# Group-major table A, column-tiled picking and a second buffer for table B in an S4 + GLU kernel

## The chip, the cores and the metric

One core of one Trainium2 chip. The metric is the device time of the kernel in microseconds (us), median over the runs. Fast runs of one kernel agree within about 1% here. Each run is put into a state (fast or slow); only fast runs are compared below. TensorE is called PE, VectorE DVE, ScalarE ACT, GpSimd POOL; "the clock" is the TensorE clock that was granted, 1.00 being full speed.

## The reference

The input is 2048 rows of 640 channels (D), with N = 128 complex states in each channel. Cut to what matters here:

```python
P = jnp.exp(logdA[:, :, None] * l[None, None, :])          # D x N x L powers
K = jnp.einsum("dn,dnl,dn->dl", Cc, P, dB).real             # the convolution's kernel, 640 x 2048
Kf, Uf = rfft2(pad(K)), rfft2(pad(u.T))
y = irfft2(Uf * Kf)[..., :L] + u * Dskip                    # u is the layer-normed input
h = x + y
out = h + (sigmoid(ln(h) @ w_gate) * (ln(h) @ w_up)) @ w_down   # D 640, F 1728
```

The change touches only how K is made.

## The kernel before

K is made in two halves of 320 channels. A tap index l is split as l = b + 8a: table B holds 21 values of b, already multiplied by C·dB, and table A holds the 32 powers of 8a. DVE builds both with chains of complex multiplies (`chain_a`, `chain_b`), the 128 states on the partitions. Then, for each group of four channels, one matrix product over the states gives every a and b at once: 128 weights (32 entries of A x 4 channels), 84 moving columns (21 entries of B x 4 channels), twice, for the real and the imaginary part. Of its result only the entries with equal channels are wanted; matmuls with one-hot weights ("picks") gather them from the evicted tile `kts` into `kv`.

```python
T["A"] = tabp.tile([P, 2, 32, w], BF16, name="tabA")        # entry, then channel; w = 320
T["B"] = tabp.tile([P, 2, 21, w], BF16, name="tabB")        # one buffer
# ... (cut)
Av = [T["A"][:, ri].rearrange("p a (c g) -> p (a c) g", c=4) for ri in range(2)]
Bv = [T["B"][:, ri].rearrange("p b (c g) -> p (b c) g", c=4) for ri in range(2)]

def product(g1, kts):                                        # kts: [P, 84, GC], GC = 20 groups
    for g0 in range(0, GC, 5):
        pk = psk.tile([P, 5, 84], F32, name="pk", tag="k")
        for i in range(5):
            for ri in range(2):
                nc.tensor.matmul(pk[:, i, :], lhsT=Av[ri][:, :, g1 + g0 + i], rhs=Bv[ri][:, :, g1 + g0 + i], ...)
        nc.scalar.copy(kts[:, :, g0:g0 + 5].rearrange("p x g -> p g x"), pk[:])

def diagonal(g1, kts):
    for c in range(4):
        # ... (cut)
        for m in range(4):                                   # 128 output columns, accumulated
            nc.tensor.matmul(pv, lhsT=pick[:, c, m, :], rhs=kts[:, 4 * m + c:4 * m + c + 65:16, :], start=(m == 0), stop=(m == 3))
        nc.tensor.matmul(ps[0:4, 1, 0:GC], lhsT=last[:, c, :], rhs=kts[:, 80 + c, :], start=True, stop=True)
        nc.scalar.copy(kvv[:, :, c, g1:g1 + GC], pv)
        nc.vector.tensor_tensor(kl[:, dc], ps[0:4, 1, 0:GC], uh[:, dc], ALU.mult)
```

Channel d is stored as (c, g) with c in 0..3 and g in 0..79, so neighbouring weights of a group lie 80 bf16 elements (160 bytes) apart, and so do neighbouring moving columns. The eviction writes each bf16 40 bytes from the last (GC = 20). The picks read `kts` in dense runs of 20.

The order of work is: tables of half 0, product of half 0, tables of half 1 with the spectrum of half 0 (`kspec`), product of half 1, spectrum of half 1, MLP.

## Time and profile before

557.67 us, median of 3 runs (555.96 to 559.83). The first view is the table of windows of the kernel before. Each line is one stretch: its length, the busy time of PE, of PE's weight loads, of DVE, ACT and POOL (in brackets the instructions), the granted clock, the DMA share and GB/s.

```profile
core 0: us, PE busy (x) PEld busy (x) DVE busy (x) ACT busy (x) POOL busy (x), PEclk, DMA share, GB/s
0.00:100.20 100.20, 31.73 (x146) 14.79 (x147) 87.13 (x144) 74.31 (x132) 20.52 (x25) 0.96 0.47 147
100.20:145.80 45.60, 40.69 (x260) 32.88 (x260) 6.75 (x26) 41.35 (x43) 0.67 (x2) 0.50 0.12 33
145.80:225.80 80.00, 51.01 (x369) 28.53 (x367) 75.72 (x98) 23.82 (x39) 0.00 (x0) 0.76 0.55 158
225.80:265.80 40.00, 37.58 (x240) 31.78 (x240) 2.42 (x16) 33.57 (x32) 0.00 (x0) 0.50 0.09 19
265.80:555.70 289.90, 251.91 (x1405) 125.81 (x1427) 122.03 (x237) 61.08 (x99) 5.20 (x8) 0.93 0.26 87
```

| stretch | what it is | what sets its length |
|---|---|---|
| 0 to 100.2 | tables of half 0, layer norm, first transform of u | DVE, 87.1 of 100.2 us busy |
| 100.2 to 145.8 | product and picking, half 0 | PE 40.7 and ACT 41.4 of 45.6 us; the clock is 0.50 |
| 145.8 to 225.8 | tables of half 1, spectrum of half 0 | DVE, 75.7 of 80 us |
| 225.8 to 265.8 | product and picking, half 1 | PE 37.6, ACT 33.6 of 40 us; the clock is 0.50 |
| 265.8 to 555.7 | spectrum of half 1, loads, MLP | not touched |

The instructions of the two products stand in these groups (line, engine, operation, tiles, shapes, count; then busy us and mean ns of one; then the idle time before them and what ended it):

```profile
L378 ACT CAST kts<-pk 128x420 bf16<-128x420 f32 x32 | 62.8, 2081 | 9.8 <-PE pk L377 9.3
L377 PE MATMUL pk<-tabB,tabA 128*128 128x84 bf16 x320 | 59.6, 353 | 11.4 <-DVE tabB L312 6.3 <-ACT kts L378 4.9
...
L385 PE MATMUL ps_kv<-kts,c_pick 128*128 128x100 bf16 x128 | 17.7, 279 | 2.1 <-DVE klast L389 2.1
```

A mean time of a matmul is not its cost, because matmuls overlap. Their cost is read from the timeline of PE, from one start to the next:

```profile
112.78 1.87 PE L377 MATMUL pk<-tabB,tabA 128*128 128x84 bf16 x10 [0.85 <-ACT kts L378]
115.50 3.73 PE L377 MATMUL pk<-tabB,tabA 128*128 128x84 bf16 x20 [0.84 <-ACT kts L378]
119.04 0.43 PE L385 MATMUL ps_kv<-kts,c_pick 128*128 128x100 bf16 x3
...
130.78 0.44 PE L385 MATMUL ps_kv<-kts,c_pick 128*128 128x100 bf16 x3
131.15 0.18 PE L386 MATMUL ps_kv<-kts,c_last 128*4 128x20 bf16 x1
131.26 0.51 PE L385 MATMUL ps_kv<-kts,c_pick 128*128 128x100 bf16 x4
131.70 0.18 PE L386 MATMUL ps_kv<-kts,c_last 128*4 128x20 bf16 x1
...
140.03 0.27 PE L385 MATMUL ps_kv<-kts,c_pick 128*128 128x100 bf16 x1
140.23 0.18 PE L386 MATMUL ps_kv<-kts,c_last 128*4 128x20 bf16 x1
```

Twenty product matmuls take 119.04 - 115.50 = 3.54 us to the next start, 177 ns each.

### The profile page before, as it was taken

The page shows a single profiled execution, that of the slowest core. Times are in us where ns is not written, and L with a number is a line of the kernel's source. Part 1 is how long each engine was busy: PE and PEld are TensorE (multiplying, and loading weights), DVE is VectorE, ACT ScalarE, POOL GpSimd, SP SyncE. Part 2 cuts the span into 40 slices and gives each one's busy share as a digit, 9 for nine tenths or more (in the row PEclk, how much of TensorE's full clock was granted, in tenths as well). Part 3 has the DMA queues.
Part 4 walks back from the last instruction along what each step waited for, and adds up shares of the span by engine and source line. Part 5 has one row for each costly group of instructions (what it writes and reads, how often), then busy time and mean ns, then how long its engine had stood idle before and what let it go on. Part 6 is the DMA issues. An engine that isn't in the chain of part 4 may idle for free.

```text
span 555.7 us, 6282 instructions
## 1 busy us (share of the span) xinstructions
PE 412.9 (74%) x2417; PEld 233.8 (42%) x2440; DVE 294.1 (53%) x518; ACT 234.1 (42%) x341; POOL 26.4 (5%) x35
## 2 busy tenths in 40 slices
PE   1201734789655885699968359799979999999997
PEld 1100212578423453587534124444444444444443
DVE  4899899400589999200653275732273236322321
ACT  5679866889601364598445203030202110311210
POOL 0721200000000000000000000000000000000000
PEclk9999998555557898555799669799988999999999
DMA  7330546500253477001798991200100010001001
GB/s 207 124 115 30 195 176 177 141 1 2 58 142 94 139 239 226 14 1 16 255 297 281 276 385 55 94 1 1 48 0 1 1 47 1 0 1 47 2 8 40
DMA packets 47725, 54.73 MB, mean 98 GB/s; under 512 B 6928, under 2 KB 39760, under 8 KB 47696
## 3 DMA queue, kind: packets, MB, share of 16 engines
q1 hardware_dynamic: 47696, 54.33, 31.3%
q8 instruction: 19, 0.31, 0.2%
q14 instruction: 10, 0.08, 0.1%
HBM read 41.21 MB, written 13.11 MB: 98 GB/s over the span
## 4 chain that ended last, share of the span: by engine, by line
PE 49%; DVE 27%; ACT 9%; DMA 9%; issue 2%; POOL 2%; SPq 1%; POOLq 0%; DVEq 0%; ACTq 0%
PE ml_pg L605 11%; PE ml_po L619 10%; PE ml_pu L605 10%; PE pk L377 7%; DVE tS L310 5%; ACT kts L378 5%; PE ps_xk L417 4%; DMA mk<-s4c_M 4%; DVE ln_st L216 3%; DVE tabB L311 3%; DVE u L235 2%; PE ps_kv L385 2%; DMA W2g<-s4c_W 2%; DVE tabB L312 2%; DVE h L478 2%
## 5 line engine op out<-in xcount | busy, mean ns | idle before, releaser
L607 ACT ACTIVATE ml_sg<-ml_pg 128x512 bf16<-128x512 f32 (+1 forms) x56 | 33.3, 597 | 120.9 <-PE ml_pg L605 120.9
L608 DVE TENSOR_TENSOR ml_hm<-ml_pu,ml_sg 128x512 bf16<-128x512 f32 (+1 forms) x56 | 38.7, 691 | 78.8 <-PE ml_pu L605 69.7
L605 PE MATMUL ml_pg<-lnT,Wg 128*128 128x512 bf16 (+1 forms) x273 | 71.3, 391 | 0.5 <-issue 0.2
L605 PE MATMUL ml_pu<-lnT,Wu 128*128 128x512 bf16 (+1 forms) x274 | 69.1, 380 | 0.5 <-issue 0.4
L377 PE MATMUL pk<-tabB,tabA 128*128 128x84 bf16 x320 | 59.6, 353 | 11.4 <-DVE tabB L312 6.3
L378 ACT CAST kts<-pk 128x420 bf16<-128x420 f32 x32 | 62.8, 2081 | 9.8 <-PE pk L377 9.3
L619 PE MATMUL ml_po<-Wd,ml_hm 128*128 128x512 bf16 (+3 forms) x438 | 64.8, 298 | 0.6 <-issue 0.2
L417 PE MATMUL ps_xk<-kv,mk 128*128 128x320 bf16 x340 | 57.2, 328 | 10.0 <-DMA mk<-s4c_M 8.9
L377 PEld LDWEIGHTS <-tabA 128*128 128x128 bf16 x320 | 50.1, 162 | 18.6 <-issue 15.4
L418 ACT CAST xk<-ps_xk 128x640 bf16<-128x640 f32 x34 | 23.5, 693 | 65.0 <-PE ps_xk L417 49.8
L417 PEld LDWEIGHTS <-mk 128*128 128x128 bf16 x340 | 34.7, 106 | 31.8 <-DMA mk<-s4c_M 11.0
L619 PEld LDWEIGHTS <-ml_hm 128*128 128x128 bf16 x448 | 33.3, 97 | 31.8 <-issue 9.0
L605 PEld LDWEIGHTS <-Wg 128*128 128x128 bf16 (+1 forms) x280 | 27.8, 101 | 35.3 <-issue 6.5
L605 PEld LDWEIGHTS <-Wu 128*128 128x128 bf16 (+1 forms) x280 | 27.6, 99 | 31.8
L389 DVE TENSOR_TENSOR klast<-ps_kv,uhead 4x20 bf16<-4x20 f32 x32 | 4.8, 166 | 65.4 <-ACT kv L387 65.4
L621 DVE TENSOR_TENSOR ml_out<-ml_po,h 128x640 bf16<-128x640 f32 x16 | 13.2, 825 | 42.8 <-PE ml_po L619 42.8
L591 ACT COPY lnT<-ml_pt 128x512 bf16<-128x512 bf16 x8 | 4.7, 586 | 61.6 <-PE ml_pt L590 61.6
L332 PEld LDWEIGHTS <-c_F_99 128*128 128x128 bf16 x64 | 8.0, 126 | 51.7 <-issue 47.5
L449 ACT CAST g_stg<-ps_g 128x640 bf16<-128x640 f32 x32 | 21.0, 699 | 10.1 <-PE ps_g L445 7.5
L352 PEld LDWEIGHTS <-W2g 128*64 128x64 bf16 x136 | 10.0, 156 | 33.4 <-DMA W2g<-s4c_W 20.1
L478 DVE TENSOR_TENSOR h<-ps_y,h 128x640 bf16<-128x640 f32 x16 | 12.8, 819 | 13.9 <-PE ps_y L474 12.7
L310 DVE TENSOR_TENSOR tS<-tabA,tabMA 128x3200 bf16<-128x3200 bf16 (+3 forms) x14 | 19.5, 1393 | 0.7 <-ACT tabA L302 0.4
(346 smaller groups left out, 547.4 us busy)
## 6 DMA issues: line engine op xcount, KB each, us to landing
mk<-s4c_M SPq DMA_DIRECT2D x34, 320.0 KB, 3.8
d1u<-s_stg SPq DMA_DIRECT2D x16, 320.0 KB, 2.6
a2g<-d1u SPq DMA_DIRECT2D x16, 320.0 KB, 3.2
W3g<-s4c_W SPq DMA_DIRECT2D x16, 192.0 KB, 3.6
u<-in_A_u_dram SPq DMA_DIRECT2D x4, 640.0 KB, 6.3
d_0_58<-g_stg SPq DMA_DIRECT2D x8, 320.0 KB, 3.6
h<-in_A_u_dram SPq DMA_DIRECT2D x4, 640.0 KB, 8.1
d_1_59<-g_stg SPq DMA_DIRECT2D x8, 320.0 KB, 4.2
```

The costliest lines, as they stand in the source:

```text
L216: nc.vector.bn_stats(st[:, r, hh, :], src[:, r, 320 * hh:320 * hh + 320])
L310: nc.vector.tensor_tensor(t, X[:, :, src, :], mm, ALU.mult)
L377: nc.tensor.matmul(pk[:, i, :], lhsT=Av[ri][:, :, g1 + g0 + i], rhs=Bv[ri][:, :, g1 + g0 + i], start=(ri == 0), stop=(ri == 1))
L378: nc.scalar.copy(kts[:, :, g0:g0 + n].rearrange("p x g -> p g x"), pk[:, 0:n, :])
L417: nc.tensor.matmul(ps[:, ri, 0:w], lhsT=mk[:, ri, j, :], rhs=kv[:, j, :], start=(j == 0), stop=(j == 4))
L418: nc.scalar.copy(xk[:, qi, :, :], ps[:, :, 0:w])
L449: nc.scalar.copy(stg[0][:, 2 * (q % 2):2 * (q % 2) + 2, :], ps[:, :, 0:w])
L478: nc.vector.tensor_tensor(hv, ps[:, :, 0:w], hv, ALU.add)
L605: nc.tensor.matmul(ps[0:fw, :], lhsT=W[:, dc, f0:f0 + fw], rhs=rhs, start=(dc == 0), stop=(dc == 4))
L607: nc.scalar.activation(sg[0:fw, :], pg[0:fw, :], AF.Sigmoid)
L608: nc.vector.tensor_tensor(hm[0:fw, ft, :], pu[0:fw, :], sg[0:fw, :], ALU.mult)
L619: nc.tensor.matmul(po[:, c0:c0 + w], lhsT=hm[0:fw, ft, 128 * lr:128 * lr + 128], rhs=Wd[0:fw, ft, c0:c0 + w], start=(ft == 0), stop=(ft == ...
```

## The change

The intent: let every access of the product be dense. A is laid out group by group, so that a group's 128 weights are side by side. B keeps its rows, but the four channels of a group become neighbours, so the moving operand comes in runs of four. The eviction then writes a group's 84 values side by side. The picking reads at steps instead (168 bytes), so it is recast: 16 matmuls with 32 output columns each, four of them beside each other in the PE array, writing PSUM at steps of 16 bytes; one eviction of 400 columns for 20 groups in place of four of 100. B gets two buffers, so that half 1's chain B can run while half 0's product still reads B. The rest of the diff regroups and reorders work: chain A does its multiplies in fewer, larger steps, the complex product C·B and some small steps of the layer norm go from POOL to DVE, the second transform of u for half 1 is evicted by ACT instead of DVE, and chain B, chain A, the spectrum and the transform are interleaved. The core of the diff:

```diff
+    bp = sc.pool("tabb", bufs=2, side="right")
...
-        T["A"] = tabp.tile([P, 2, 32, w], BF16, name="tabA")
-        T["B"] = tabp.tile([P, 2, 21, w], BF16, name="tabB")
+        A = T["A"] = tabp.tile([P, 2, w // 4, 32, 4], BF16, name="tabA")
+        T["B"] = bp.tile([P, 2, 21, HALVES[hf][1]], BF16, name="tabB", tag="B")
...
-                        nc.tensor.matmul(pk[:, i, :], lhsT=Av[ri][:, :, g1 + g0 + i], rhs=Bv[ri][:, :, g1 + g0 + i], ...)
-                nc.scalar.copy(kts[:, :, g0:g0 + n].rearrange("p x g -> p g x"), pk[:, 0:n, :])
+                        nc.tensor.matmul(pk[:, i, :], lhsT=A[:, ri, g].rearrange("p e c -> p (e c)"), rhs=B[:, ri, :, 4 * g:4 * g + 4], ...)
+                nc.scalar.copy(kts[:, g0:g0 + 5, :], pk[:])
...
-                for m in range(4):
-                    nc.tensor.matmul(pv, lhsT=pick[:, c, m, :], rhs=kts[:, 4 * m + c:4 * m + c + 65:16, :], start=(m == 0), stop=(m == 3))
-                nc.scalar.copy(kvv[:, :, c, g1:g1 + GC], pv)
+                for m in range(4):
+                    nc.tensor.matmul(pv[32 * m:32 * m + 32, :, :, c], lhsT=pick[:, c, :], rhs=kj[:, :, :, 4 * m + c], start=True, stop=True,
+                                     tile_position=(0, 32 * m))
+            nc.scalar.copy(kv[:, :, 4 * g1:4 * g1 + 4 * GC], ps[:, 0, 0:20 * GC].rearrange("p (j x) -> p j x", j=5))
...
+    open_b(1)
+    nc.scalar.copy(T["B"][:, :, 0, :], CB1[:])
+    kv = kmm(0, ktp, kx, T0)
+    cb = chain_b(1)
+    drain(cb, 4)
+    ks, s2 = kspec(0, kv, xu0, kw2, mkp, False), u_s2(1, xu1, a2p, nc.scalar.copy)
+    for _ in range(5):
+        drain(cb, 1); drain(ks, 1); drain(s2, 1)
...
```

## The prediction

> **What bounds the kernel now.** From 337 us on (219 us) it is the MLP: PE 94% busy at clock 0.97 (table of windows); the change does not touch it. Before, by windows and timeline:
> - 0–100 us: VectorE (DVE) builds tables A and B of half 0, busy for 87 of 100 us; the first product waits for the last tabB add (100.3).
> - 100–145 and 226–266: products and diagonal picking. Ten product matmuls take 1.87 us, the ACT eviction of each five groups 2.08 us (128x420, written at steps of 40 bytes; a dense 128x640 takes 0.69). The two leapfrog at clock 0.50. DVE does 6.5 and 1.2 us of work: idle.
> - 145–226: DVE builds half 1, evicts u_s2 (17 at 0.82 us) and multiplies the spectrum: 76 of 81 us busy. It sets the start of the second product.
> - 266–316: spectrum of half 1, waiting on mk loads.
>
> **What the change does.**
> 1. Product: a group's 128 weights are dense, B comes in runs of four, the eviction is dense: 0.55 us (estimate from 0.69). A dense pair (picking, 100 columns) takes 0.112 us at clock 0.5 today, so I estimate 1.1 us per ten matmuls. Sixteen blocks per half: 18 us.
> 2. Picking: still 20 matmuls per block of 20 groups, now 32-column tiles side by side, reading SBUF at steps of 168 bytes and writing PSUM at 16. Today 2.2 us. The Trainium skill (Advanced Engine Details and Errata, Memory Cachelines) says non-contiguous PSUM patterns slow matmuls; no trace here shows how much. I take 2.5 us, tiles overlapping. With it a half takes about 29 us, against 45 and 40.
> 3. Chain A keeps its elements (28 us by today's durations) if runs of four bf16 keep two elements per cycle. The skill (Vector Engine (DVE) Microarchitecture Reference, 5.1 and 5.2) asks for an innermost step of one and runs of 8 bytes; these satisfy it.
> 4. B in two buffers: about 11 us of half 1's chain B moves under the first product; not more, because the DVE queue holds four klast multiplies that wait for the picking. The u_s2 eviction (13 us) moves to ACT, which has room. The 81 us become about 58: 12 chain B, 2.5 bases, 28 chain A, 13 spectrum, waits.
> 5. Front: GpSimd work that stretched eight u normalisations to 8.75 us (the later eight: 2.94) goes; but CB moves to DVE (about 7 us) and half 1's B bases come earlier. Net about zero.
>
> **Sum.** First product 99, its end 128, second product 186, its end 215 (now 265.7): 50 us saved, all on the critical path. Spectrum of half 1, weight loads and MLP follow unchanged (290 us).
>
> Predicted 508 us, range 492 to 528. Faster by over 2%: 0.94; within 2%: 0.04; slower: 0.02.
>
> **What the profile would show.** Step 1: kts eviction 0.5–0.6 us, ten matmuls about 1.1 us, no wait of PE on ACT. Step 2: picking block 2–3 us. Step 3: DVE 2240- and 2560-element multiplies near 1.3 and 1.5 us. Step 4: DVE busy in the first product; second product near 186, released by the last tabA add. Step 5: u normalisation near 0.37 us each. MLP 219 us.
>
> **What would make it wrong.** Chain A at one element per cycle: plus 25 us per half, which eats the gain. Picking serialised by PSUM steps: plus up to 25 us. A clock above 0.5 in the denser product: minus up to 14. The spectrum of half 0 with u_s2 (about 13 MB of loads and stores) DMA-bound in 58 us.

## The result and the profile after

The changed kernel takes 470.38 us, median of 4 runs (467.87 to 471.65); the kernel before in the same rounds 557.85 us. The ratio is 0.843 (95% interval 0.838 to 0.847). A ratio here is the mean time of one kernel's fast runs over that of the other's fast runs of the same rounds, so it is not quite the ratio of the medians quoted. The prediction had the direction right and the size wrong: 470 us lies 22 us below the low end of its range.

The windows of the changed kernel, cut at the same events:

```profile
core 0: us, PE busy (x) PEld busy (x) DVE busy (x) ACT busy (x) POOL busy (x), PEclk, DMA share, GB/s
0.00:95.40 95.40, 33.53 (x159) 15.35 (x159) 85.89 (x166) 76.74 (x135) 4.83 (x10) 0.78 0.51 160
95.40:109.50 14.10, 13.73 (x238) 11.11 (x239) 10.88 (x18) 9.24 (x19) 0.67 (x2) 0.77 0.11 34
109.50:164.50 55.00, 42.83 (x370) 26.29 (x370) 54.97 (x80) 32.74 (x51) 0.00 (x0) 0.93 0.77 230
164.50:179.00 14.50, 13.43 (x240) 10.66 (x241) 1.88 (x4) 9.14 (x19) 0.00 (x0) 0.81 0.02 5
179.00:469.30 290.30, 249.83 (x1405) 124.76 (x1428) 122.94 (x241) 61.57 (x99) 4.41 (x4) 0.94 0.26 89
```

| stretch | before | predicted | after | missed by |
|---|---|---|---|---|
| to the first product | 100.2 | 99 | 95.4 | 3.6 |
| first product | 45.6 | 29 | 14.1 | 14.9 |
| half 1's tables, spectrum of half 0 | 80.0 | 58 | 55.0 | 3.0 |
| second product | 40.0 | 29 | 14.5 | 14.5 |
| the rest | 289.9 | 290 | 290.3 | 0.3 |

So 29 of the 38 us lie in the two products. The groups that answer to those of before:

```profile
L401 PE MATMUL pk<-tabB,tabA 128*128 128x84 bf16 x320 | 19.2, 230 | 6.5 <-DVE tabA L333 4.6 <-DVE tabA L334 1.9
L401 PEld LDWEIGHTS <-tabA 128*128 128x128 bf16 x320 | 17.0, 116 | 10.7 <-issue 10.0
L403 ACT CAST kts<-pk 128x420 bf16<-128x420 f32 x32 | 15.4, 511 | 12.1 <-PE pk L401 11.7
...
L412 PE MATMUL ps_kv<-kts,c_pick 128*32 128x100 bf16 x128 | 9.4, 362 | 0.0
```

The eviction fell from 2.08 to 0.51 us, and PE no longer waits for it. PE's timeline of the first product:

```profile
95.77 4.39 PE L401 MATMUL pk<-tabB,tabA 128*128 128x84 bf16 x58 [0.94 <-DVE tabA L334]
100.09 0.54 PE L412 MATMUL ps_kv<-kts,c_pick 128*32 128x100 bf16 x5
100.57 1.52 PE L401 MATMUL pk<-tabB,tabA 128*128 128x84 bf16 x20
102.01 0.74 PE L412 MATMUL ps_kv<-kts,c_pick 128*32 128x100 bf16 x11
...
103.54 0.54 PE L412 MATMUL ps_kv<-kts,c_pick 128*32 128x100 bf16 x5
104.01 0.93 PE L401 MATMUL pk<-tabB,tabA 128*128 128x84 bf16 x20
104.87 0.74 PE L412 MATMUL ps_kv<-kts,c_pick 128*32 128x100 bf16 x11
105.23 0.34 PE L415 MATMUL ps_kv<-kts,c_last 128*4 128x20 bf16 x4
105.54 0.92 PE L401 MATMUL pk<-tabB,tabA 128*128 128x84 bf16 x20
106.39 0.54 PE L412 MATMUL ps_kv<-kts,c_pick 128*32 128x100 bf16 x5
```

The first 58 product matmuls take 100.09 - 95.77 = 4.3 us (74 ns each) and the next twenty 102.01 - 100.57 = 1.44 us (72 ns each); the later ones take 104.87 - 104.01 = 0.86 us for 20 (43 ns each, the switch to the picks included). In between the clock rises: the clock log in the trace changes from 0.50 to 1.00 at 101.9 us. In the second product it changes at 170.1 us, so that there only the first 58 run at half rate. The starts of the two five-pick groups, 103.54 and 106.39, are one block of 20 groups apart: 2.85 us. Of that, 40 product matmuls are 1.71 us, and 16 picks with four `last` matmuls are 1.14 us.

### The profile page after: what moved, and what is told of

The parts are those of the page before. It is cut to its first block, busy times and chain, and to the rows that moved or that the text cites. A ratio compares the mean times of both kernels' runs of the same rounds, so it can differ in the third digit from the quotient of the medians.

```text
span 469.3 us, 6215 instructions
## 1 busy us (share of the span) xinstructions
PE 353.4 (75%) x2412; PEld 188.2 (40%) x2435; DVE 276.6 (59%) x506; ACT 189.4 (40%) x323; POOL 9.9 (2%) x16
## 4 chain that ended last, share of the span: by engine, by line
PE 38%; DVE 35%; issue 14%; DMA 9%; ACT 2%; POOL 1%; SPq 1%; POOLq 0%; DVEq 0%
PE ml_pg L656 10%; PE ml_po L670 9%; PE ml_pu L656 9%; DMA mk<-s4c_M 4%; PE pk L401 4%; DVE tabA L332 4%; DVE tS L330 4%; PE ps_xk L446 3%; DVE ln_st L250 3%; DVE tabB L347 2%; DVE tS L346 2%; DVE tabA L334 2%; DVE tabA L333 2%; DMA g_1_2622<-d_1_59 2%; PE ps_kv L412 1%
## 5 line engine op out<-in xcount | busy, mean ns | idle before, releaser
L658 ACT ACTIVATE ml_sg<-ml_pg 128x512 bf16<-128x512 f32 (+1 forms) x56 | 33.4, 597 | 121.2 <-PE ml_pg L656 119.6
L446 PE MATMUL ps_xk<-kv,mk 128*128 128x320 bf16 x340 | 50.9, 303 | 14.1 <-DMA mk<-s4c_M 10.6
L670 PEld LDWEIGHTS <-ml_hm 128*128 128x128 bf16 x448 | 33.3, 98 | 31.8 <-issue 9.0
L446 PEld LDWEIGHTS <-mk 128*128 128x128 bf16 x340 | 32.8, 98 | 31.6 <-DMA mk<-s4c_M 13.7
L401 PE MATMUL pk<-tabB,tabA 128*128 128x84 bf16 x320 | 19.2, 230 | 6.5 <-DVE tabA L333 4.6
L401 PEld LDWEIGHTS <-tabA 128*128 128x128 bf16 x320 | 17.0, 116 | 10.7 <-issue 10.0
L403 ACT CAST kts<-pk 128x420 bf16<-128x420 f32 x32 | 15.4, 511 | 12.1 <-PE pk L401 11.7
L332 DVE TENSOR_TENSOR tabA<-tabA 128x2240 bf16<-128x2240 bf16 (+2 forms) x16 | 18.9, 1194 | 0.0
L381 PEld LDWEIGHTS <-W2g 128*64 128x64 bf16 x136 | 8.3, 132 | 25.9 <-DMA W2g<-s4c_W 9.6
L330 DVE TENSOR_TENSOR tS<-tabA 128x2240 bf16<-128x2240 bf16 (+2 forms) x16 | 18.4, 1194 | 0.0
```

Source lines behind the costliest of these rows:

```text
L330: V(t[:, ri], A[:, ri, :, s0:s1, :], bc(A[:, 1, :, b:b + 1, :], [P, G, n, 4]), ALU.mult)
L332: V(A[:, ri, :, d0:d1, :], A[:, ri, :, s0:s1, :], bc(A[:, 0, :, b:b + 1, :], [P, G, n, 4]), ALU.mult)
L401: nc.tensor.matmul(pk[:, i, :], lhsT=A[:, ri, g].rearrange("p e c -> p (e c)"), rhs=B[:, ri, :, 4 * g:4 * g + 4], start=(ri == 0), stop=(r ...
L403: nc.scalar.copy(kts[:, g0:g0 + 5, :], pk[:])
L446: nc.tensor.matmul(ps[:, ri, 0:w], lhsT=mk[:, ri, j, :], rhs=kv[:, j, :], start=(j == 0), stop=(j == 4))
L658: nc.scalar.activation(sg[0:fw, :], pg[0:fw, :], AF.Sigmoid)
```

## The experiments

Twelve runs, all with correct results. All ratios are to the kernel before in the same rounds, and every difference of time below is read against the two measurements of the changed kernel, 470.38 us (first) and 468.69 us (second, run c1_changed_again). The table gives the stretches of each run's windows in us, cut at its own events. The diffs of this section are cut to their core (`...`).

| run | time | to first product | first product | between | second product | rest |
|---|---|---|---|---|---|---|
| changed kernel | 470.4 | 95.4 | 14.1 | 55.0 | 14.5 | 290.3 |
| e1 weights strided | 478.1 | 96.1 | 19.2 | 56.2 | 19.3 | 286.9 |
| e2 moving operand strided | 508.1 | 99.8 | 32.4 | 54.1 | 32.4 | 288.0 |
| e3 eviction strided | 507.2 | 94.7 | 33.4 | 57.1 | 33.3 | 285.0 |
| e7 all three | 521.0 | 100.9 | 36.9 | 57.4 | 36.8 | 287.6 |
| e5 full-width picks | 484.6 | 94.8 | 22.4 | 53.7 | 23.1 | 289.0 |
| e6 dense PSUM | 466.1 | 94.6 | 14.1 | 55.0 | 14.7 | 284.2 |
| b1 before, dense eviction | 561.3 | 99.4 | 46.4 | 80.2 | 43.2 | 290.2 |
| s1 one buffer of B | 475.8 | 94.7 | 13.9 | 63.6 | 14.4 | 287.2 |
| s2 eviction on DVE | 481.9 | 94.5 | 14.1 | 68.4 | 14.1 | 289.1 |
| v1 early loads | 459.3 | 94.6 | 14.3 | 55.0 | 14.1 | 279.0 |
| v3 early loads, warm PE | 457.2 | 97.2 | 12.5 | 54.8 | 12.3 | 276.9 |

The last column varies by some 6 us among kernels whose work there is the same, so differences of that size in the total are not explained below; the stretches are.

### e1, e2, e3: one stride put back at a time

e1 gives A its old layout (entry, then channel), and with it the weights their 160-byte steps:

```diff
-        A = T["A"] = tabp.tile([P, 2, w // 4, 32, 4], BF16, name="tabA")
+        A = T["A"] = tabp.tile([P, 2, 32, w], BF16, name="tabA")
...
-   lhsT=A[:, ri, g].rearrange("p e c -> p (e c)")
+   lhsT=A[:, ri].rearrange("p e (c g) -> p (e c) g", c=4)[:, :, g]
```

> The changed kernel, but table A entry-major as before, so the 128 weights of a group lie 160 bytes apart; B runs, dense eviction and column-tiled picking stay. Theory W (the strided weight load was the slow part of the old product): the pair goes from 0.044 back to about 0.187 us, the first product stage from 14.1 to about 37 us, clock 0.5. Theory M (the strided moving operand was): the pair stays near 0.044 us and the stage near 14 us. Chain A as long as now; the bases may cost 2 to 3 us more on VectorE per half (strided writes), which is not the question.

478.11 us (2 runs, ratio 0.860). Twenty product matmuls take 1.73 us in place of 0.86, at a clock of 1.00; the mean weight load goes from 116 to 196 ns. A product matmul thus goes from 43 to 87 ns, not to the 187 that theory W expected and not unchanged, as theory M had it. Strided weights cost 5 us per product, the least of the three strides.

e2 gives B its old channel order, and so the moving operand its 160-byte steps:

```diff
-   rhs=B[:, ri, :, 4 * g:4 * g + 4]
+   rhs=B[:, ri].rearrange("p b (c g) -> p (b c) g", c=4)[:, :, g]
```

> The changed kernel, but B stored channel-major within the half, so that the 84 moving elements lie 160 bytes apart; weights dense. Theory M: pair about 0.187 us, stage about 37 us, clock 0.5. Theory W: pair near 0.044 us, stage near 14 us. If each adds a part, the two runs split the 0.143 us between them.

508.05 us (2 runs, ratio 0.914). The two product windows of e2, columns as above:

```profile
99.80:132.20 32.40, 31.65 (x240) 22.35 (x241) 12.67 (x18) 9.62 (x19) 0.67 (x2) 1.00 0.00 1
...
186.30:218.70 32.40, 31.66 (x240) 22.33 (x241) 1.75 (x4) 9.62 (x19) 0.00 (x0) 0.50 0.02 3
```

The same 58 matmuls in its timeline, in the first product and in the second:

```profile
101.01 9.76 PE L403 MATMUL pk<-tabB,tabA 128*128 128x84 bf16 x58 [0.75 <-DVE tabA L336]
...
187.51 9.76 PE L403 MATMUL pk<-tabB,tabA 128*128 128x84 bf16 x58 [0.74 <-DVE tabA L336]
```

A product matmul takes 168 ns (9.76 us for 58) in both products, near theory M's 187. The clock of the second product is 0.50. The 1.00 printed for the first is not a measurement: e2's clock log starts only at 132.5 us, after that product, and a stretch without a log entry is printed as 1.00. (The same holds for the whole first product of e7 and for the beginning of the first product in e1, e5, s1, s2 and v1; in s1, whose log starts at 99.7 us, the first 58 matmuls take 4.06 us under a printed 1.00, the half rate of the changed kernel.) So e2 shows the price of the stride at half clock: 168 ns, 2.0 ns for each of 84 columns, where the changed kernel's dense matmul takes 74 ns at the same 0.50. That full clock would not lower it is shown below by strided picks (e5 and b1), not by the product. The strided moving operand costs 18 us per product.

e3 gives the eviction its old 40-byte steps, while the product stays dense:

```diff
-            kts = ktp.tile([P, GC, 84], BF16, name="kts")
+            kts = ktp.tile([P, 84, GC], BF16, name="kts")
...
-                nc.scalar.copy(kts[:, g0:g0 + 5, :], pk[:])
+                nc.scalar.copy(kts[:, :, g0:g0 + 5].rearrange("p x g -> p g x"), pk[:])
```

> The changed kernel with the old eviction layout alone (groups innermost, writes 40 bytes apart); weights and B as changed. Theory E (ACT's 2.04 us per five groups set the old pace, and the waiting kept the clock at 0.5): stage at least 16 x 2.04 = 33 us, clock 0.5, pair near 84 columns / 1.2 GHz = 0.070 us inside a block. If the strided write is cheaper than in the old trace (because PE no longer reads with strides at the same time): eviction clearly under 2 us. The picking then reads dense runs of 20: if its 168-byte read steps cost anything now, the 16 picks take less than their 0.53 us.

507.24 us (2 runs, ratio 0.912). Its timeline of PE:

```profile
100.64 0.86 PE L401 MATMUL pk<-tabB,tabA 128*128 128x84 bf16 x10 [0.98 <-ACT kts L403]
102.48 0.86 PE L401 MATMUL pk<-tabB,tabA 128*128 128x84 bf16 x10 [0.98 <-ACT kts L403]
```

Ten matmuls take 0.86 us, then PE waits 0.98 us for ACT: a new set of five groups every 1.84 us, which is ACT's pace. The clock is 0.50 in both products. Theory E holds. So with only the eviction strided a product takes 33 us, as long as with only the moving operand strided. The two were separate limits at nearly the same height. Removing either alone could not have brought the gain.

### e7: all three strides at once

The edits of e1, e2 and e3 together, in one kernel; picks, buffers and order of work stay as in the changed kernel.

> The changed kernel with all three old layouts of the product together (table A entry by entry, B channel by channel, eviction written at steps of 40 bytes), the rest of the change kept: column-tiled picks, second B buffer, order of the work. It splits the gain of 87 us into layout and the rest. Theory: the limits of the products coincide and do not add (each of moving operand and eviction alone gave 32 to 33 us), so the products take 32 to 37 us each and the kernel 507 to 517 us, that is 37 to 47 us for the layouts, the remaining 40 to 50 for picking, buffer and schedule. Rival (the losses of the three single runs, 8 + 38 + 37 us, add up): about 550 us.

521.0 us (6 runs, ratio 0.935). The three single losses are 8, 38 and 37 us; together they are 51 (52 in the same rounds as c1). They do not add, as the theory said, although 521 is above its 507 to 517. The products lie inside what was expected (36.9 and 36.8 us); the miss is in the front, where DVE, which also has to write the bases of A and B in the old order, is busy for 91.5 us in place of 85.9 and the first product starts at 100.9 us.

This splits the whole gain of 88.4 us in these rounds (557.13 - 468.69). Putting the layouts back costs 52 us: 45 in the products (73.7 against 28.5 in c1) and 6 in the front, where the way in which e7 writes its bases may be to blame and not the layout as such. The other 36 us (557.13 - 521.0) are 22.6 us in the stretch between the products (80.0 to 57.4) and 11.9 us in the products themselves (85.6 to 73.7), where e7 keeps the new picking and the one large eviction of `kv`. A further 2.3 us lie in the rest, which varies by as much, and e7's longer front takes 0.7 back.

### b1: the dense eviction alone, on the kernel before

```diff
-            kts = ktp.tile([P, 84, GC], BF16, name="kts")
+            kts = ktp.tile([P, GC, 84], BF16, name="kts")
...
-   rhs=kts[:, 4 * m + c:4 * m + c + 65:16, :]
+   rhs=kts[:, :, 4 * m + c:4 * m + c + 65:16].rearrange("p g j -> p j g")
```

> The kernel before with the eviction alone made dense (picks then read SBUF at steps of 168 bytes). Theory: a strided product pair is limited by the reading of the moving operand at 170 to 187 ns, so ten take 1.7 to 1.9 us whether or not the eviction waits; the two products go from 45.6 and 40.0 us to about 37 to 40 each, kernel 548 to 556 us. Rival: the eviction was the limit and the matmuls only followed it, so ten matmuls fall to 0.9 us or less and the products to about 20 us each, kernel about 510 to 515 us.

561.28 us (4 runs, ratio 1.006, interval 1.002 to 1.010): slightly slower, by less than 1%. The rival (the eviction is the limit) is out. The theory had the pace of the product right, ten matmuls in 1.7 to 1.9 us as before, but it missed that the picks become strided: four picks and the `last` now take 0.98 us from start to next start, where before they took 0.55. The stride had not been removed, only moved from ACT's write to PE's read. Its price can be read off three picks and one, each up to the switch:

```profile
128.21 0.75 PE L385 MATMUL ps_kv<-kts,c_pick 128*128 128x100 bf16 x3
128.90 0.20 PE L386 MATMUL ps_kv<-kts,c_last 128*4 128x20 bf16 x1
...
138.42 0.37 PE L385 MATMUL ps_kv<-kts,c_pick 128*128 128x100 bf16 x1
138.72 0.20 PE L386 MATMUL ps_kv<-kts,c_last 128*4 128x20 bf16 x1
```

Two picks more take 0.69 - 0.30 = 0.39 us, 195 ns each, at a logged clock of 0.50.

### e5: the old full-width picks in the changed kernel

```diff
-   nc.tensor.matmul(pv[32 * m:32 * m + 32, :, :, c], lhsT=pick[:, c, :], rhs=kj[:, :, :, 4 * m + c], start=True, stop=True, tile_position=(0, 32 * m))
+   nc.tensor.matmul(pv[:, :, :, c], lhsT=pick[:, c, 96 - 32 * m:224 - 32 * m], rhs=kj[:, :, :, 4 * m + c], start=(m == 0), stop=(m == 3))
...
```

> The changed kernel with the old picking: 128 output columns, four accumulating matmuls for each channel, in place of 16 column tiles of 32; all else dense as in the changed kernel (one of three weight buffers of the spectrum is given up to make room for the wider table, which should cost nothing). Theory: a pick costs its 100 columns over the clock either way (42 ns at full clock, 83 at half), so 16 picks take 0.7 to 1.3 us against 0.74 us of the tiled ones; kernel 0 to 5 us more. Rival (column tiles run side by side and that is where the picking gained): 16 picks 2 us or more, plus 8 us or more for the kernel.

484.58 us (4 runs, ratio 0.868): 14 us slower than the changed kernel. The theory (a pick costs its columns over the clock either way) is wrong, the rival right. The timeline of PE:

```profile
105.19 0.94 PE L401 MATMUL pk<-tabB,tabA 128*128 128x84 bf16 x20
105.96 2.63 PE L412 MATMUL ps_kv<-kts,c_pick 128*128 128x100 bf16 x13
108.53 0.32 PE L414 MATMUL ps_kv<-kts,c_last 128*4 128x20 bf16 x4
```

Thirteen picks take 108.53 - 105.96 = 2.57 us, 198 ns each: 100 columns at a step of 168 bytes, again 2.0 ns for each column, at full clock (e5's log shows 1.00 from 98.7 to 167.0 us). b1's strided picks take 195 ns at 0.50, so this price does not depend on the clock; and b1 writes PSUM densely where e5 writes it at 16-byte steps, so PSUM does not set it. Sixteen of them are 3.2 us of a block. In the changed kernel the same sixteen reads, as 32-column tiles, and the four `last` matmuls together take 1.14 us. Four tiles side by side cost about what one full-width matmul with the same strided read costs. The Trainium skill (TensorEngine Tiling (Array Packing), Key Properties) says that tiles operate independently; this is its size here. Column tiling did not only save matmul work, it hid most of the stride that the dense eviction had moved into the picks. Not all: e3's sixteen tiled picks, which read dense runs, take 0.54 us at half clock, the changed kernel's 0.74 us at full clock. The trace of e5 shows one thing more: before full-width picks twenty product matmuls take 105.96 - 105.19 = 0.77 us, 38 ns each. The 0.86 us of the changed kernel are 0.09 us more, which goes with the switch to the 32-column tiles.

### e6: a dense PSUM write in the picks

```diff
-            pv = ps[:, 0, 0:20 * GC].rearrange("p (j g c) -> p j g c", j=5, c=4)
+            pv = ps[:, 0, 0:20 * GC].rearrange("p (j c g) -> p j c g", j=5, c=4)
```

with the reordering moved into the evictions to `kv` and `klast`.

> The changed kernel, but each pick writes 20 adjacent PSUM words (channel-major) and ACT permutes while evicting. Theory P (PSUM steps of 16 bytes slow the matmul, as the prediction feared): 16 picks fall clearly under the present 0.53 us (33 ns each), toward 100 columns over four concurrent tiles. Rival: steps in PSUM cost nothing here, picks stay at 33 ns each, and the kv eviction alone gets longer than 0.49 us.

466.06 us (2 runs, ratio 0.838, interval 0.829 to 0.848). The blocks are 2.85 us apart, as in the changed kernel, the eviction of `kv` takes 492 ns in both, and the products are 14.1 and 14.7 us. The 16-byte step in PSUM cost nothing that shows. The total is 4 us lower, nearly all of it in the rest of the kernel, which the edit does not touch and which varies by as much. One limit of this test: the picks read SBUF at steps, and a smaller PSUM penalty could hide under that (b1 against e5 above speaks against it for full-width picks).

### s1 and s2: the schedule undone, one part at a time

s1 builds half 1's table B in the buffer that the first product reads:

```diff
-    T0 = dict(T)
-    open_b(1)
-    nc.scalar.copy(T["B"][:, :, 0, :], CB1[:])
-    kv = kmm(0, ktp, kx, T0)
+    kv = kmm(0, ktp, kx, dict(T))
+    nc.scalar.copy(T["B"][:, :, 0, :], CB1[:])
```

> The changed kernel, but half 1's table B is built in the one buffer that half 0's product still reads, so chain B of half 1 starts only when the first product is over. Theory (prediction step 4: the second buffer moves chain B under the first product): the 10.9 us that DVE works in the first product leave its shadow, the stage between the products grows from 55 us to 62 to 66, the first product stays near 14 us, kernel 478 to 482 us. Rival (the products shrank so far that the overlap is worth little, or DVE has idle time elsewhere to take it up): under 3 us more than the changed kernel.

475.76 us (4 runs, ratio 0.853), 5.4 us slower. The stretch between the products grew by 8.6 us to 63.6, within what was expected; DVE works only 2.8 us in the first product in place of 10.9. The total is a little below the expected 478 because the rest took 287.2 us in place of 290.3. The rival (under 3 us) is out.

s2 puts the eviction of half 1's transform back on DVE:

```diff
-   u_s2(1, xu1, a2p, nc.scalar.copy)
+   u_s2(1, xu1, a2p, nc.vector.tensor_copy)
```

> The changed kernel with the 17 evictions of u_s2 of half 1 back on DVE (0.74 to 0.82 us each in the traces, 13 us). Theory: between the products DVE is busy all of 55 us and sets the time, so the stage grows to about 66 to 69 us and the kernel to 480 to 485 us. Rival: the stage is as much bound by DMA (0.77 busy) or PE, so it grows by less than 5 us.

481.86 us (4 runs, ratio 0.863), 11.5 us slower; the stretch between the products is 68.4 us with DVE busy for 67.5. As expected: this stretch is DVE's, and what is taken off DVE there comes off the kernel, 13.4 us of the stretch for seventeen evictions.

### c1, v1 and v3: two steps further

Two things were left. In the second product the DMA engines stand still (DMA share 0.02), and after it PE waits 10 us for loads of `mk`, the tiles of the matrix that turns `kv` into its spectrum. And PE enters each product at a clock of 0.50. v1 loads the first eight `mk` tiles into the buffer that `xu0` has just left, before the second product. v3 adds 44 spare matmuls on entries of A that are ready one step earlier, so that PE is busy ahead of the product, and takes the `klast` multiply (of what the `last` matmuls picked with rows of u) off DVE:

```diff
+    pt = kx.tile([P, 17, 2, HALVES[0][1]], BF16, name="mkpre", tag="xu0")        # v1 and v3
+    pre = [... eight slices of 1280 columns, each loaded by sy.dma_start(v, cd["M"][QORD[k]]) ...]
     kv = kmm(1, ktp, kx, dict(T))
...
+        wt = psk.tile([P, 256], F32, name="warm", tag="k")                          # v3 only
+        for i in range(44):
+            nc.tensor.matmul(wt[:], lhsT=ident[:], rhs=A[:, 0, 0:16, 17:21, :].rearrange("p g e c -> p g (e c)"), start=True, stop=True)
-            nc.vector.tensor_tensor(kl[:, dc], ps[0:4, 1, 0:4 * GC], uh[:, dc], ALU.mult)
+            nc.scalar.copy(kl[:, dc], ps[0:4, 1, 0:4 * GC])
+            nc.gpsimd.tensor_tensor(kl[:, dc], kl[:, dc], uh[:, dc], ALU.mult)
```

> The changed kernel itself, as the measure for the two runs after it in the same rounds: 468 to 472 us.

468.69 us (6 runs, 466.4 to 471.4).

> The changed kernel, and the first eight mk tiles of half 1's spectrum are loaded into the freed buffer of xu0 before the second product, in which the DMA engines are idle (DMA share 0.00 to 0.05 for 14.5 us). Theory: from the second product to the MLP the time is set by the amount of loading (DMA share 0.8 to 1.05 from 185 to 245 us), and 2.6 MB at about 300 GB/s is 8.7 us; kernel 4 to 10 us faster than the changed one, 460 to 466 us, and PE waits on mk fall from 10 us to under 3. Rival: a chain of dependent steps sets this stretch, not the bytes: within 2 us.

459.31 us (6 runs, 458.6 to 461.3), 9.4 us below c1; the ratios to the kernel before are 0.824 (interval 0.822 to 0.827) and 0.841 (0.837 to 0.844), which do not touch. The second product's DMA share is 0.45 now and the rest is 279.0 us in place of 286.5. The waits of PE for `mk` fell from 10.0 to 6.1 us, not to under 3 as expected: in its trace the queue issues seven loads of Wg and Wu (178.9 to 192.6 us) ahead of the ninth `mk` (196.5).

> As the run before, and two things more: 44 spare 256-column matmuls on table A just ahead of each product, so that PE does not stand idle before it; and the klast multiply no longer on DVE (ACT copies, GpSimd multiplies). Theory: the first 58 matmuls of a product ran at a clock of 0.50 because PE had been idle (4.4 us in place of about 2.5), so warm they take about 2.5 us, 1.9 us less per product; DVE's 3 us of waiting for klast in the first product go too. Together 3 to 7 us faster than the prefetch alone. Rival: the clock falls again in the gap before the last add of table A, and the first 58 still take over 4 us.

457.2 us, median of 6 runs (454.4 to 464.1); two of the six were slow. The fast ones give a ratio of 0.818 (0.815 to 0.822) against v1's 0.824 (0.822 to 0.827): about 3 us faster than v1, with intervals that touch. Its timeline of PE at the first and the second product:

```profile
94.95 2.47 PE L423 MATMUL warm<-tabA,c_ident 128*128 128x256 bf16 x21
97.26 1.15 PE L401 MATMUL pk<-tabB,tabA 128*128 128x84 bf16 x20
98.67 0.94 PE L401 MATMUL pk<-tabB,tabA 128*128 128x84 bf16 x20 [0.26 <-ACT kts L403]
...
100.68 0.54 PE L412 MATMUL ps_kv<-kts,c_pick 128*32 128x100 bf16 x5
...
159.97 4.76 PE L423 MATMUL warm<-tabA,c_ident 128*128 128x256 bf16 x42
164.58 0.92 PE L401 MATMUL pk<-tabB,tabA 128*128 128x84 bf16 x20
...
167.73 0.54 PE L412 MATMUL ps_kv<-kts,c_pick 128*32 128x100 bf16 x5
```

The warm theory holds in its direction: the first sixty product matmuls take 3.42 and 3.15 us, where the changed kernel takes 4.3 us for 58, and the products are 12.5 and 12.3 us, with the clock logged at 1.00 in both windows. They do not take the expected 2.5 us, because PE now waits for ACT's evictions in between. In the first product the gain was lost again: the spare matmuls were still running at 97.26 us, so the product began about 1.5 us later than in the changed kernel (95.77). Against v1 the front is 2.6 us longer, each product 1.8 us shorter and the rest 2.1 us shorter, which is within the variation of that column; what v3's two additions are worth is therefore about 1 us and not clear of noise. v3 has the lowest median found.

## Why the prediction was right or wrong

**Step 1, the product: wrong in size, and the main miss.** The prediction said: "A dense pair (picking, 100 columns) takes 0.112 us at clock 0.5 today, so I estimate 1.1 us per ten matmuls. Sixteen blocks per half: 18 us." The 0.112 was four picks divided into 0.445 us, and that time contains the switch to the 4-column matmul. Taken apart as shown above, a dense matmul was 0.083 us at half clock, its 100 columns over 1.2 GHz. Measured after: 0.74 us per ten at half clock, 0.43 at full clock. In the first product 78 matmuls ran at the first rate and 82 at the second, 9.3 us (4.3 + 1.44 + 82 x 0.043); in the second product 58 and 102, 8.7 us (4.3 + 102 x 0.043). That is 8.7 and 9.3 us less than the 18.

**The clock.** The prediction kept 0.5 throughout and named a higher clock only as a risk worth "minus up to 14". It rose in both products, 6.1 us after the 58 dense matmuls began in the first (95.8 to 101.9) and 4.3 us after in the second (165.8 to 170.1). The Trainium skill (TensorE: Matmul & The Clock Gate, Part 1) says that the clock is halved by default and released by about 3.4 us of sustained activity. The traces agree roughly: over the changed kernel and the variants in which it rose, the rise came 2.8 us (s2's second product, 178.3 to 181.1) to 6.1 us after the 58 began, and v3's spare matmuls, begun at 89.2 us, were followed by a logged rise at 92.7, ahead of the product. But a PE that the profile shows as busy was not enough: wherever the log covers a product with the moving operand strided, the clock stays at 0.50 to the end, in both products of the kernel before, both of b1 (PE 46.1 of 46.4 us busy in the first), the second of e2 (31.7 of 32.4 us) and the second of e7. With the weights alone strided (e1) it rose. Why, no run settles.

**Step 2, picking: wrong in size.** Predicted 2.5 us for 20 groups; measured 1.14, so 5.4 us less per half (4 x 1.36). The prediction took today's 2.2 us and added a little for the strides. Two errors of opposite sign stood behind this: today's 2.2 us contain four switches of 0.12 us, and strided full-width picks would have taken 3.2 us (e5); and tiles side by side cut even those to 1.14 with the `last` matmuls. It also quoted the skill (Advanced Engine Details and Errata, Memory Cachelines) on non-contiguous PSUM patterns; e6 shows no such cost here. The cost of the same section that fits what did count, a different SBUF line at each access, was on the other operand; that lines are the cause of the 2.0 ns was not tested.

Together, 8.7 + 5.4 = 14.1 us in the first product and 9.3 + 5.4 = 14.7 in the second, against the 14.9 and 14.5 us of the table above; 0.8 us of the first stays open.

**The limit before: right, but not taken apart.** "The two leapfrog" is borne out: e2 and e3 give 32 and 33 us for either alone. The prediction did not say what held ten matmuls at 1.87 us (177 ns each from start to start). It was the stride of the moving operand, neither the low clock nor the weights: at a logged 0.50 that stride alone gives 168 ns (e2, second product), strided weights alone 83 ns (e1, 4.81 us for 58 in the second product), a dense matmul 74 ns.

**Step 3, chain A: right.** The 2240- and 2560-element multiplies took 1.32 and 1.49 us against the predicted 1.3 and 1.5. Runs of four bf16 kept the rate of the old dense multiply (3200 elements in 1.82 us), as the skill led to expect (Vector Engine (DVE) Microarchitecture Reference, 5.1 and 5.2).

**Step 4, the schedule: right, 3 us short.** 58 us predicted, 55.0 measured with DVE busy for 54.97. The two parts were expected to be worth 11 and 13 us; s1 shows 8.6 us and s2 13.4 us in that stretch. The four `klast` multiplies did hold DVE, but only for 3 us.

**Step 5, the front: 3.6 us short.** Net zero was predicted and 4.8 us gained: DVE's busy time fell by 1.2 us and its idle time from 13.1 to 9.5. The sixteen u normalisations went from 802 to 440 ns on average, 5.7 us in all, which the C·B product on DVE partly used up. How the gain divides over POOL's work going, C·B and the new order was not tested.

**The rest: right.** 290 predicted, 290.3 measured.

## What to carry to other kernels

Before a cost is scaled from today's trace, take one instruction out of its mixture: fit two or three counts (one, three and four picks) and see whether the slope is columns over the clock; what remains is a fixed cost that the new code may not pay. Look at every operand's step, moving, weights, eviction and picks: on PE a moving operand with a wide step cost about 2 ns a column here (at both clocks for the picks), runs of four bf16 run near the clock's rate (38 to 43 ns for 84 columns), and where a step cannot be avoided, column tiles side by side share its cost. When two engines run at nearly the same pace, expect little from relieving one (b1) and much from relieving both. And before a printed clock is trusted, compare it with the pace of a dense matmul in the same stretch: e2's 1.00 was a stretch without a log.

## What the Trainium skill lacked or had wrong

- Advanced Engine Details and Errata, Memory Cachelines (SBUF): it states a penalty when each access falls on another line, without a size. Here a moving operand at 160-byte steps takes 168 ns for 84 columns and one at 168-byte steps 198 ns for 100 columns, against 38 to 43 ns for 84 columns in runs of four bf16; and for the picks the cost is the same at a clock of 1.00 (e5, 198 ns) and of 0.50 (b1, 195 ns).
- The same section, for weights: nothing. Weights at 160-byte steps double a product matmul to 87 ns, and the mean load goes from 116 to 196 ns.
- The same section (PSUM): "Any non-contiguous AP significantly slows down matmuls". Not seen: picks that write at 16-byte steps and picks that write densely both give blocks of 2.85 us, and full-width picks take 198 ns with such steps (e5) and 195 ns without (b1), though the picks' strided SBUF reads could hide a small cost.
- ScalarE: Activation LUTs has no figure for a strided write. A 128x420 eviction from PSUM written at 40-byte steps takes 2.08 us on average (one every 1.84 us in e3), written densely 0.51.
- TensorEngine Tiling (Array Packing): it says that a change of mode drains the array, without a time. From a full-width pick to a 4-column matmul it was about 0.12 us, and from the product to 32-column picks about 0.09; whether these are such changes no run tells. It also does not say that tiles share a strided read: 16 tiled picks and four small matmuls take 1.14 us where 16 full-width picks take 3.2.
- TensorE: Matmul & The Clock Gate, Part 1: no page says why a product with PE 98% busy stays at 0.50 for 32 us (e2, second product), as the products with a strided moving operand did here.
